# A transformer block on one core: the second norm's tiles turned by DMA in place of TensorE

## The chip, the cores and the metric

The kernel runs on one core of a Trainium2 chip. The metric is the device time of one execution in microseconds (us), the median of several runs. Five engines work side by side, each through its own in-order list of instructions: TensorE (PE; its weight loads are shown apart as PEld), VectorE (DVE), ScalarE (ACT), GpSimd (POOL), and SyncE (SP), which here does nothing but issue DMAs, one after the other.

## The reference, cut to what matters

One pre-norm transformer block in bf16: 2048 rows, width 512, 32 heads of 16, a gated feed-forward of width 1792.

```python
x = A_x                                   # (1, 2048, 512)
h = x + attention(layernorm(x), A_wqkv, A_wo)
h2 = h + glu(layernorm(h))                # the second norm
# glu(y) = (sigmoid(y @ w_gate) * (y @ w_up)) @ w_down
```

`layernorm` subtracts the row's mean and divides by the root of its variance plus 1e-5, with no weights.

## The kernel before, in words

The 2048 query rows are cut into five chunks: chunks 0, 1 and 2 of 512 rows, chunks 3 and 4 of 256. Attention is one long loop of 683 numbered steps. A step computes scores of three (chunk, head group, key block, head) units on PE (line 876) into one of two PSUM buffers `pss`, takes their exponential (line 887, ACT; in some steps VectorE does a third of them by a bit trick, lines 905 to 920), and some steps later multiplies by the values (line 958) into the accumulator `acc`. The keys lie in `KT`, the query rows of a head group in one of two buffers `QB`.

When a head group of a chunk is done, `emit_norm` (line 927) divides by the row sums through a chain of DMAs, all issued by SP: VectorE copies `acc` to `xs` (932), four DMAs take the sums to DRAM (`sd`, 935), one brings them back spread over the partitions (`s_all`, 936), VectorE takes the reciprocal (943) five or six steps later, one DMA writes it to DRAM (`rd`, 945), four broadcast it (`rb_all`, 947), and VectorE multiplies ten or eleven steps after the start (939, into `OT`). SP also issues, in program order between these, the query rows of the next head group (`emit_q_rows`, line 238, four DMAs, and their bounds `bnd`, line 248, two), the loads of x (`xr`, 598) and the output (640). An SP instruction that waits holds up all that stand behind it.

Beside attention, a Python generator `filler()` yields small pieces of other matmul work, which `emit_fill` (line 973) puts behind the scores of chosen steps: `("at", n)` means the next step that is n modulo 4, `("gap", n)` leaves n steps free, `("from", n)` waits for step n. `later(i, fn)` has `fn` emitted at step i. The order of all engines is written out this way; no scheduler changes it.

For chunks 0 to 3 the filler does, while the following chunk's attention runs, the output projection, the second norm and the feed-forward (`ffn_tasks`):

- `ffn_wo` (chunks 0, 1) or `ffn_wo_tight` (chunks 2, 3) takes a tile of 128 rows at a time: eight matmuls (`wo_mm`, line 593) into a `pm` tile, then `wo_ln`, which adds x (602), takes mean and variance (145, 146), has the root taken on POOL (152) and emits the normalization `ln_apply` (156, VectorE) two steps later into the bf16 tile `hn` (tag `xn`, two buffers).
- `hn_transpose` turns the tile: `transpose4` writes four 128x128 transposes by PE (162) into a `pm` tile, and VectorE copies them to `hnT` (163). In the attention phase `pm` has one PSUM buffer, shared by all fillers.
- `ffn_up` multiplies `hnT` by the gate and up weights (617), with a tanh on ACT (622) and a product on VectorE (630). The first gate group reads `hnT` of all the chunk's tiles. `ffn_down` (633, 638) makes the output.

By the built order, the tiles of chunk 0 are turned at steps 193, 201, 209 and 217 and its first gate group stands at step 219; chunk 1: 365, 373, 381, 389 and 391; chunk 2: 533, 537, 541, 545 and 547; chunk 3: 641, 645 and 647. The last chunk (`ffn_last`, after the loop) turns its two tiles by itself (line 786).

Of the kernel before, what the change touches and what calls it, by code (L numbers as in the profile page):

```python
# [19 lines left out]
def kernel(  # L20
# [11 lines left out]
    nc = tc.nc  # L32
    P = 128
# [6 lines left out]
    NG = H // 4  # L40
# [30 lines left out]
    def pm_tile():  # L71
        return pmh["pool"].tile([P, 512], FP32, name="pm")
# [13 lines left out]
    for part in (1, 0, 2):  # L86
        nc.sync.dma_start(out=wqkv_sb[:, :, part * D:(part + 1) * D],
                          in_=wqkv_v[:, :, part * D:(part + 1) * D])
# [3 lines left out]
    hnT = reg[:, o1:o1 + DC * QC].rearrange("p (c q) -> p c q", c=DC)  # L92
# [50 lines left out]
    def ln_stats(src, mv):  # L143
        st = small.tile([P, nc.vector.BN_STATS_DIM], FP32, name="st")
        nc.vector.bn_stats(out=st[:], in_=src)
        nc.vector.bn_aggr(out=mv, in_=st[:])

    def ln_rstd(mvs, n):
        ve = small.tile([P, n], FP32, name="ve")
        nc.vector.tensor_scalar(out=ve[:], in0=mvs[:, :, 1], scalar1=1e-5, scalar2=None, op0=ALU.add)  # L150
        rs = small.tile([P, n], FP32, name="rs")
        nc.gpsimd.tensor_tensor(out=rs[:], in0=ve[:], in1=pw_neg[:, 0:n], op=ALU.pow)  # L152
        return rs

    def ln_apply(dst, src, mv, rs):
        nc.vector.tensor_scalar(out=dst, in0=src, scalar1=mv[:, 0:1], scalar2=rs,
                                op0=ALU.subtract, op1=ALU.mult)

    def transpose4(dst3, src, copy=None):
        pt = pm_tile()[:].bitcast(BF16)[:, 0:4 * P].rearrange("p (b q) -> p b q", b=4)  # L160
        for b in range(4):
            nc.tensor.transpose(out=pt[:, b, :], in_=src[:, b * P:(b + 1) * P], identity=ident_bf[:])
        (copy or nc.vector.tensor_copy)(out=dst3, in_=pt)
# [423 lines left out]
    def tiles_of(c):  # L587
        q0, w = CHUNKS[c]
        return range(q0 // P, (q0 + w) // P)

    def wo_mm(ps, c, tt, g):
        assert ("o", c, g) in ready
        nc.tensor.matmul(ps[:], lhsT=OT[c % 2][:, g, tt * P:(tt + 1) * P], rhs=wo_pad[:, g, :],  # L593
                         start=(g == 0), stop=(g == NG - 1))

    def x_load(t):
        xr = pmh.get("work", work).tile([P, D], BF16, name="xr")
        nc.sync.dma_start(out=xr[:], in_=x_v[:, t, :])
        return xr

    def wo_ln(ps, xr, tt):
        nc.vector.tensor_tensor(out=h_sb[:, tt, :], in0=ps[:], in1=xr[:], op=ALU.add)
        mv = small.tile([P, 1, nc.vector.BN_AGGR_DIM], FP32, name="mv")
        ln_stats(h_sb[:, tt, :], mv[:, 0, :])
        rs = ln_rstd(mv, 1)
        hn = pmh.get("work", work).tile([P, D], BF16, name="xn", tag="xn")
        later(state["step"] + 2, lambda: ln_apply(hn[:], h_sb[:, tt, :], mv[:, 0, :], rs[:, 0:1]))
        return hn

    def hn_transpose(tt, hn, copy=None):  # L610
        transpose4(hnT[:, :, tt * P:(tt + 1) * P], hn, copy)

    def blocks_of(w):
        return [tuple(range(f, f + QC // w)) for f in range(0, FC, QC // w)]
# [24 lines left out]
                                       op0=ALU.mult, op1=ALU.add)  # L639
        nc.sync.dma_start(out=out_v[:, t, :], in_=ob[:])  # L640

    def ffn_wo(c):
        for tt, t in enumerate(tiles_of(c)):
            xr = x_load(t)
            yield ("at", 3)
            ps = pm_tile()
            for g in range(NG):
                if g == NG // 2:
                    yield ("at", 1)
                yield 1  # L650
                wo_mm(ps, c, tt, g)
            hn = wo_ln(ps, xr, tt)
            yield ("gap", 1)
            yield ("at", 1)
            yield 1
            hn_transpose(tt, hn)

    def ffn_wo_tight(c):
        turn = None
        for tt, t in enumerate(tiles_of(c)):  # L660
            xr = x_load(t)
            yield ("at", 3)
            ps = pm_tile()
            for g in range(NG):
                if g == NG // 2:
                    yield ("at", 0)
                yield 1
                wo_mm(ps, c, tt, g)
            hn = wo_ln(ps, xr, tt)
            if turn:  # L670
                yield ("at", 1)
                yield 1
                hn_transpose(*turn)
            turn = (tt, hn)
        yield ("gap", 1)
        yield ("at", 1)
        yield 1
        hn_transpose(*turn)

    def ffn_up(c):  # L680
        w = CHUNKS[c][1]
        at = cycle((3, 1) if c + 2 < NC else (3, 0, 1))
        for fs in blocks_of(w):
            yield ("at", next(at))
            psg = pm_tile()
            for i, f in enumerate(fs):
                for k in range(DC):
                    yield w / QC
                    ffn_mm(wg, psg, w, f, i, k)
            sg = gate_act(psg)  # L690
            yield ("at", next(at))
            psu = pm_tile()
            for i, f in enumerate(fs):
                for k in range(DC):
                    yield w / QC
                    ffn_mm(wu, psu, w, f, i, k)
            up_mul(psu, sg, fs, w)

    def ffn_down(c, tight):
        at = 0  # L700
        for tt, t in enumerate(tiles_of(c)):
            for f in range(FC):
                if tight:
                    if f % 3 == 0:
                        yield ("at", (3, 0, 1)[at % 3])
                        at += 1
                elif f % 5 in (0, 3):
                    yield ("at", 0 if f % 5 else 3)
                if f == 0:
                    psd = pm_tile()  # L710
                yield 1
                down_mm(psd, f, tt)
            down_out(psd, t, tt)

    def ffn_tasks(c):
        tight = c + 3 >= NC
        yield ("rate", 8.0)
        yield from (ffn_wo_tight if tight else ffn_wo)(c)
        yield from ffn_up(c)
        yield from ffn_down(c, tight)  # L720
        yield ("rate", None)
        yield ("gap", 1)
# [102 lines left out]
    def filler():  # L825
        for t in range(NV0, NT):
            yield from fill_v(t)
        for b in range(1, 4):
            yield from fill_k(b)
            yield from fill_q0(b)  # L830
        for qc in range(1, NQC):
            yield from fill_q(qc)
        for c in range(NC - 1):
            yield ("from", int(first_step(c + 1)) + (11 if c + 3 >= NC else 15))
            yield from ffn_tasks(c)
        yield from wo_early(NC - 1)
# [129 lines left out]
    def later(i, fn):  # L966
        due.setdefault(i, []).append(fn)
# [3 lines left out]
    state = {"wait": 0, "debt": 0.0, "done": False, "next": 0, "rate": None}  # L971
# [135 lines left out]
```

## Time and profile before

| | |
|---|---|
| median of 3 runs | 961.85 us (961.81 to 962.77) |
| profiled execution | 963.82 us |
| its span, first to last instruction | 962.0 us |
| mean granted TensorE clock | 0.996 of full |
| the 56 transposes of the fillers (line 162) | 219 ns median each as recorded, pipelined; one group of four 0.38 to 0.40 us |
| the 14 copies (line 163) | 418 ns median each |
| the 14 normalizations (line 156) | 541 ns median each |

A profile line of a timeline reads: start, length, engine, line of the kernel, operation, output<-input, how many; in brackets the idle time of the engine just before and what ended it. A line of a window table reads: start:end of the stretch, its length, then the busy time (and count) of PE, PEld, DVE, ACT and POOL, the granted clock, the DMA share and GB/s. "SPq" is SP issuing a DMA: the duration is that of the issue. In the chain, a piece "DMA" is the time from an issue's start until the work it released went on. Times of a timeline are counted from the span's start.

### The profile page before, as it was taken

The page shows a single profiled execution, that of the slowest core. Times are in us where ns is not written, and L with a number is a line of the kernel's source. Part 1 is how long each engine was busy: PE and PEld are TensorE (multiplying, and loading weights), DVE is VectorE, ACT ScalarE, POOL GpSimd, SP SyncE. Part 2 cuts the span into 40 slices and gives each one's busy share as a digit, 9 for nine tenths or more (in the row PEclk, how much of TensorE's full clock was granted, in tenths as well). Part 3 has the DMA queues.
Part 4 walks back from the last instruction along what each step waited for, and adds up shares of the span by engine and source line. Part 5 has one row for each costly group of instructions (what it writes and reads, how often), then busy time and mean ns, then how long its engine had stood idle before and what let it go on. Part 6 is the DMA issues. An engine that isn't in the chain of part 4 may idle for free.

```text
span 962.0 us, 17291 instructions
## 1 busy us (share of the span) xinstructions
PE 843.0 (88%) x6442; PEld 337.0 (35%) x6442; DVE 782.9 (81%) x1413; ACT 898.6 (93%) x778; POOL 39.8 (4%) x56
## 2 busy tenths in 40 slices
PE   5998888878888999998788999988788999998988
PEld 2321222222222232222222223222355545456646
DVE  7488888888788888899888888898898778777643
ACT  6789999999999999999999999999998999999862
POOL 4600000000000000000000000000000000000000
PEclk9998999999999999999999999999999999999999
DMA  5102450000003000001001000000010000110010
GB/s 161 24 1 56 115 117 16 16 16 3 15 26 103 16 16 17 19 14 30 9 26 27 16 17 15 19 10 27 16 31 23 17 10 16 27 32 16 9 35 12
DMA packets 37645, 28.45 MB, mean 30 GB/s; under 512 B 17788, under 2 KB 32920, under 8 KB 37560
## 3 DMA queue, kind: packets, MB, share of 16 engines
q1 hardware_dynamic: 37416, 27.22, 10.8%
q8 instruction: 50, 0.82, 0.4%
q14 instruction: 35, 0.29, 0.1%
q10 hardware_dynamic: 144, 0.13, 0.0%
HBM read 20.31 MB, written 2.61 MB: 24 GB/s over the span
## 4 chain that ended last, share of the span: by engine, by line
PE 45%; DVE 22%; ACT 22%; issue 6%; DMA 3%; SPq 1%; POOL 0%; ACTq 0%; DVEq 0%
PE pss L876 21%; ACT pt L887 13%; PE acc L958 8%; PE pm L617 7%; ACT stg L887 4%; ACT wd L887 3%; DVE stg L906 2%; PE pm L633 2%; ACT QTu L887 2%; PE pm L593 2%; DVE pt L919 2%; DVE y L915 2%; PE pm L166 1%; DVE reg L909 1%; DVE reg L630 1%
## 5 line engine op out<-in xcount | busy, mean ns | idle before, releaser
L876 PE MATMUL pss<-QB,KT 128*128 128x512 bf16 (+3 forms) x2554 | 477.5, 338 | 80.2 <-ACT pt L887 40.6
L887 ACT ACTIVATE pt<-pss 128x1536 bf16<-128x1536 f32 (+1 forms) x392 | 502.3, 1364 | 17.1 <-PE pss L876 10.6
L876 PEld LDWEIGHTS <-KT 64*128 64x128 bf16 (+1 forms) x2554 | 179.4, 95 | 341.4 <-issue 233.5
L887 ACT ACTIVATE stg<-pss 128x1536 bf16<-128x1536 f32 (+1 forms) x140 | 183.3, 1359 | 5.0 <-PE pss L876 3.8
L906 DVE TENSOR_SCALAR stg<-pss 128x512 int32<-128x512 f32 x123 | 84.8, 690 | 68.2 <-PE pss L876 60.5
L958 PE MATMUL acc<-pt,Vaug 128*17 128x512 bf16 (+1 forms) x1471 | 112.7, 338 | 2.3 <-DVE pt L919 1.2
L887 ACT ACTIVATE wd<-pss 128x1536 bf16<-128x1536 f32 (+1 forms) x80 | 103.9, 1387 | 3.0 <-PE pss L876 2.6
L887 ACT ACTIVATE QTu<-pss 128x1024 bf16<-128x1024 f32 (+1 forms) x71 | 95.7, 1348 | 1.7 <-PE pss L876 1.3
L912 DVE SCALAR_TENSOR_TENSOR y<-reg 128x512 f32<-128x512 f32 x123 | 85.2, 692 | 4.2
L915 DVE SCALAR_TENSOR_TENSOR y<-y,reg 128x512 f32<-128x512 f32 x123 | 84.3, 685 | 1.1
L958 PEld LDWEIGHTS <-Vaug 128*17 128x17 bf16 x2560 | 49.3, 89 | 95.6 <-issue 81.3
L617 PE MATMUL pm<-reg,reg 128*128 128x512 bf16 (+1 forms) x280 | 57.9, 337 | 7.6 <-DVE reg L630 7.5
L617 PE MATMUL pm<-reg,wu 128*128 128x512 bf16 (+1 forms) x280 | 58.1, 338 | 1.4 <-ACT sg L622 1.1
L633 PE MATMUL pm<-wd,reg 128*128 128x512 bf16 x196 | 55.6, 382 | 1.9 <-DVE ob L638 1.9
L909 DVE TENSOR_SCALAR reg<-stg 128x512 int32<-128x512 int32 x123 | 51.9, 422 | 1.8
L958 PE MATMUL acc<-stg,Vaug 128*17 128x256 bf16 (+1 forms) x564 | 50.6, 326 | 0.7 <-DVE stg L919 0.7
L630 DVE SCALAR_TENSOR_TENSOR reg<-sg,pm 128x512 bf16<-128x512 f32 x56 | 38.2, 683 | 14.2 <-PE pm L617 13.8
L919 DVE SCALAR_TENSOR_TENSOR pt<-y,stg 128x512 bf16<-128x512 f32 x70 | 48.0, 686 | 2.0
L152 POOL TENSOR_TENSOR rs<-ve,pw_neg 128x1 f32<-128x1 f32 x16 | 11.7, 734 | 881.9 <-DVE ve L150 875.3
L622 ACT ACTIVATE sg<-pm 128x512 f32<-128x512 f32 x56 | 36.3, 649 | 10.2 <-PE pm L617 9.8
L906 DVE TENSOR_SCALAR wd<-pss 128x512 int32<-128x512 f32 x45 | 31.0, 689 | 17.0 <-PE pss L876 15.5
L171 PE MATMUL pm<-reg 128*128 128x512 bf16 x124 | 38.2, 397 | 1.4 <-DVE stg L521 0.7
(149 smaller groups left out, 718.0 us busy)
## 6 DMA issues: line engine op xcount, KB each, us to landing
rb_all<-rd SPq DMA_DIRECT2D x96, 64.0 KB
xr<-in_A_x_dram SPq DMA_DIRECT2D x16, 128.0 KB
out_dram<-ob SPq DMA_DIRECT2D x15, 128.0 KB
rb_all<-rd SPq DMA_DIRECT2D x60, 32.0 KB
reg<-in_A_x_dram SPq DMA_DIRECT2D x7, 256.0 KB
KT<-stg SPq DMA_DIRECT2D x7, 256.0 KB
reg<-in_B_w_gate_dram SPq DMA_DIRECT2D x4, 448.0 KB
wu<-in_B_w_up_dram SPq DMA_DIRECT2D x4, 448.0 KB
```

The lines of the kernel that those rows point to most:

```text
L171: nc.tensor.matmul(ps[:], lhsT=wqkv_sb[:, c, w0:w0 + P], rhs=xnT[:, c, n * QC:(n + 1) * QC], start=(c == 0), stop=(c == DC - 1))
L617: nc.tensor.matmul(ps[:, i * w:(i + 1) * w], lhsT=wt[:, c, f * P:(f + 1) * P], rhs=hnT[:, c, 0:w], start=(c == 0), stop=(c == DC - 1))
L630: nc.vector.scalar_tensor_tensor(out=out, in0=a, scalar=1.0, in1=b, op0=ALU.add, op1=ALU.mult)
L633: nc.tensor.matmul(ps[:], lhsT=hT[:, f, tt * P:(tt + 1) * P], rhs=wd[:, f, :], start=(f == 0), stop=(f == FC - 1))
L876: nc.tensor.matmul(pss[:, ui, h * w:(h + 1) * w], lhsT=KT[rows, g, kt * P:(kt + 1) * P], rhs=QB[n_qg % 2][rows, j, 0:w], start=True, stop= ...
L887: ex = nc.scalar.activation(out=pt[:, 0:na, :], in_=pss[:, 0:na, :], func=ACT.Exp, scale=DH ** -0.5 / QS)
L906: return nc.vector.tensor_scalar(out=e_bits, in0=src, scalar1=ONE_BITS, scalar2=0.0, op0=ALU.add, op1=ALU.max)
L909: nc.vector.tensor_scalar(out=e_man, in0=e_bits, scalar1=0x7FFFFF, scalar2=-0x40800000, op0=ALU.bitwise_and, op1=ALU.bitwise_or)
L912: nc.vector.scalar_tensor_tensor(out=e_pol, in0=m, scalar=PA, in1=m, op0=ALU.add, op1=ALU.mult)
L915: nc.vector.scalar_tensor_tensor(out=e_pol, in0=e_pol, scalar=PB, in1=e_man.bitcast(FP32), op0=ALU.add, op1=ALU.mult)
L919: nc.vector.scalar_tensor_tensor(out=dst, in0=e_pol, scalar=PC, in1=e_bits.bitcast(FP32), op0=ALU.add, op1=ALU.mult)
L958: nc.tensor.matmul(acc[32 * j:32 * j + VW, 0:w], lhsT=Vaug[:, kt, 4 * g + j, :], rhs=p[:, h * w:(h + 1) * w], start=(kt == 0), stop=(kt == ...
```

## The change

The four transposes of a tile on PE and the copy by VectorE are replaced by four DMAs from SBUF to SBUF that transpose on the way. They are issued by SP, emitted three steps after `wo_ln`, one step after the normalization. `hn_transpose` goes, and with it the filler's waits for its place; the two variants of `ffn_wo` become one. Chunks 0 and 1 leave two free steps after each tile, and every chunk three before the feed-forward. The last chunk and the first norm are not changed.

```diff
         hn = pmh.get("work", work).tile([P, D], BF16, name="xn", tag="xn")
+
+        def turn():
+            for b in range(4):
+                nc.sync.dma_start(out=hnT[:, b, tt * P:(tt + 1) * P], in_=hn[:, b * P:(b + 1) * P], transpose=True)
+
         later(state["step"] + 2, lambda: ln_apply(hn[:], h_sb[:, tt, :], mv[:, 0, :], rs[:, 0:1]))
-        return hn
-
-    def hn_transpose(tt, hn, copy=None):
-        transpose4(hnT[:, :, tt * P:(tt + 1) * P], hn, copy)
+        later(state["step"] + 3, turn)
...
-    def ffn_wo(c):
+    def ffn_wo(c, tight):
         for tt, t in enumerate(tiles_of(c)):
             xr = x_load(t)
             yield ("at", 3)
             ps = pm_tile()
             for g in range(NG):
                 if g == NG // 2:
-                    yield ("at", 1)
+                    yield ("at", 0 if tight else 1)
                 yield 1
                 wo_mm(ps, c, tt, g)
-            hn = wo_ln(ps, xr, tt)
-            yield ("gap", 1)
-            yield ("at", 1)
-            yield 1
-            hn_transpose(tt, hn)
-
-    def ffn_wo_tight(c):
...
+            wo_ln(ps, xr, tt)
+            if not tight:
+                yield ("gap", 2)
+        yield ("gap", 3)
...
-        yield from (ffn_wo_tight if tight else ffn_wo)(c)
+        yield from ffn_wo(c, tight)
```

By the built order of the changed kernel, the transposing DMAs stand on SP at these places: chunk 0, tile 2 directly ahead of the query rows of the next head group; chunk 2, tile 0 ahead of an `rd`, tile 1 ahead of an `xr` and an `sd`, tiles 2 and 3 between `s_all` and `rd`; chunk 3, tile 0 ahead of an `rd`, tile 1 between the next group's `s_all` and its `rd`. The first gate group of chunk 0 moves from step 219 to 223 and that of chunk 1 from 391 to 395; those of chunks 2 and 3 stay at 547 and 647. Lines behind the change move up by 21 in the changed kernel (876 becomes 855).

More of the change, by code (lines that the diff above doesn't have):

```diff
@@ L648, in ffn_wo @@
                 if g == NG // 2:
-                    yield ("at", 1)
+                    yield ("at", 0 if tight else 1)
                 yield 1
                 wo_mm(ps, c, tt, g)
-            hn = wo_ln(ps, xr, tt)
-            yield ("gap", 1)
-            yield ("at", 1)
-            yield 1
-            hn_transpose(tt, hn)
-    def ffn_wo_tight(c):
[L659 to L678, printed above, removed]
+            wo_ln(ps, xr, tt)
+            if not tight:
+                yield ("gap", 2)
+        yield ("gap", 3)
     def ffn_up(c):
```

## The prediction

> **What bounds the kernel now.** I read the page's busy shares first, then its chain, then windows and timelines around the 14 turned tiles.
>
> ```profile
> PE 843.0 (88%) x6442; PEld 337.0 (35%) x6442; DVE 782.9 (81%) x1413; ACT 898.6 (93%) x778; POOL 39.8 (4%) x56
> PE 45%; DVE 22%; ACT 22%; issue 6%; DMA 3%; SPq 1%; POOL 0%; ACTq 0%; DVEq 0%
> ```
>
> No engine alone is the bound: ScalarE (ACT) is 93% busy, and the chain goes through TensorE (PE), VectorE (DVE) and ACT, since two score buffers tie them together. So the answer differs by stage. Windows of one four-step cycle show it (columns: length, then busy us of PE, PEld, DVE, ACT, POOL).
>
> ```profile
> 289.80:294.70 4.90, 4.63 (x32) 1.60 (x32) 3.57 (x8) 4.90 (x5) 0.00 (x0) 1.00 0.37 89
> 716.70:722.60 5.90, 5.25 (x61) 3.21 (x60) 5.46 (x14) 5.29 (x6) 0.59 (x1) 1.00 0.17 44
> 722.60:729.50 6.90, 5.65 (x62) 3.12 (x61) 6.16 (x13) 5.12 (x4) 0.70 (x1) 1.00 0.12 28
> 729.50:734.90 5.40, 4.49 (x56) 2.76 (x55) 5.13 (x11) 5.00 (x4) 0.97 (x1) 1.00 0.02 2
> ```
>
> In chunk 0 (first row, with one turned tile) ACT is busy 4.90 of 4.90: whatever PE and DVE save there is hidden. In chunk 2 two cycles are 0.5 and 1.5 us longer than the 5.4 of their neighbour, with ACT idle.
>
> **What goes.** 56 PE transposes and 14 DVE copies (418 ns each, 5.9 us). The view of line 162 gives the transposes' waits as 4.4 + 2.0 + 1.4 + 0.4 + 0.2 = 8.4 us, and the timeline shows 0.38 to 0.40 us for each group of four, 5.6 us in all. On the path is only what ACT waits for:
>
> ```profile
> 727.09 1.02 PE L593 MATMUL pm<-wo_pad,OT 128*128 128x512 bf16 x4 [1.01 <-DVE reg L163]
> 729.52 1.02 ACT L887 ACTIVATE pt<-pss 128x1024 bf16<-128x1024 f32 x1 [1.42 <-PE pss L876]
> ```
>
> PE waits 1.01 us for the copy of line 163 to give back the one PSUM buffer `pm`, and ACT then idles 1.42 us. I count the chunk-2 excess, 0.5 + 1.5 less 0.1 that ACT needs anyway: 1.9 us gained. In chunks 0 and 1 nothing is gained, since ACT covers it; what could be late next there is ACT itself. In chunk 3 the saved PE time only runs into the wait below, so 0.
>
> **What is moved.** In the built order the FFN of chunks 0 and 1 starts four steps later (219 to 223, 391 to 395) and still ends at steps 324 and 496, ahead of the next filler at 359 and 527. Steps are shifted, not added: 0. If that cover fails, one bad meeting with another task costs the difference between FFN cycles, 6.0 (326.0 to 332.0) against 5.4. FFN steps of chunks 2 and 3 stay.
>
> **What comes.** 56 transposing DMAs of 128x128, four a tile, on SP's in-order queue. No row shows one. Let T be the time from one to the next, whether SP is held or the transfers follow one another, and let the last land 1.40 us after it starts (the chain's piece DMA rd from 736.17). T's lower end is SP's cheapest issue, 0.22 (line 935); the upper end is 1.85, the chain's piece DMA rb_all from 738.87, if each waits out the one before. Nearer rows are the dearest plain issue, 0.62 (line 248: 1.25 for two), and 1.40, a small DMA issued and landed. It cuts more pieces than the former and should not need a full round trip each, so I take their middle, **T = 1.0**. In the Trainium skill, "VectorE: DVE Perf Modes", section "The three transpose paths", a DMA transpose of this tile is put at 1309 ns against 390 on TensorE; no run here shows it, and by it the sum below would be +23.6 instead of +15.6.
>
> SP itself has time for 56 T. What matters is who stands behind them and who waits. Three places come out of the new SP order.
>
> *Place 1, chunk 0.* Tile 2's transposes wait for its normalization (line 156, 300.03 + 0.54), and the next head group's query rows now stand behind them. Before, SP ran ahead:
>
> ```profile
> 292.73 2.48 SPq L238 DMA_DIRECT2D QB<-QTu  x4
> 295.25 1.25 SPq L248 DMA_DIRECT2D QB<-bnd  x2
> 302.15 5.27 ACT L887 ACTIVATE pt<-pss 128x1536 bf16<-128x1536 f32 x4
> ```
>
> The first bound row now lands at 300.57 + 4T + 2.52 + 1.40 = 304.5 + 4T. Step 213's scores need it; its exp is the fourth of the last row, at 302.15 + 3/4 x 5.27 = 306.1, and scores take 0.6. Loss: 4T - 1.0, so 3.0 us. In chunk 1 the rows behind tile 1's transposes would land at 512.9 (end of rb) + 4T + 0.4 (xr) + 2.5 + 1.4 = 521.2, 0.6 of scores ahead of their step's exp at 525.22: some 3 us to spare, 0.
>
> *Place 2, chunk 2.* The order is tile 0's four, rd, rb, QB, tile 1's four, xr, sd, s_all, tile 2's four, tile 3's four. Tile 0's start at 716.11 (line 156), so rd goes at 720.1 instead of 717.68 and everything behind is 2.4 late: tile 1's from 725.16 + 2.4 = 727.6 to 731.6, sd at 732.0 with xr's 0.4 (before: 727.40), s_all done 2.45 later, tile 2's from 734.4, tile 3's from 738.4, the last landed at 738.4 + 3 + 1.4 = 742.8. The first gate matmuls (line 617, 738.15) need it by 738.15 + 0.65. So the chunk ends 4.0 late, the 1.9 gain swallowed; below T of about 0.7 nothing is lost and part of the 1.9 stays.
>
> *Place 3, chunk 3.* Here tile 1's transposes stand behind s_all, which waits for sd to land, which stands behind rb and QB:
>
> ```profile
> 867.75 0.32 SPq L945 DMA_DIRECT2D rd<-r_all  x1
> 869.19 2.20 SPq L947 DMA_DIRECT2D rb_all<-rd  x4
> 871.43 2.47 SPq L238 DMA_DIRECT2D QB<-QTu  x4
> 873.96 1.25 SPq L248 DMA_DIRECT2D QB<-bnd  x2
> 875.31 1.24 SPq L935 DMA_DIRECT2D sd<-xs_all  x4
> 877.42 0.34 SPq L936 DMA_DIRECT2D s_all<-sd  x1
> 875.75 1.05 PE L617 MATMUL pm<-reg,reg 128*128 128x256 bf16 x8
> ```
>
> The last row is the first gate group, which reads both tiles: it runs before s_all is even issued, so these transposes come late whatever they cost. rd waits for tile 0's (866.19 + 4T = 870.2, was 867.75), tile 1's start 10.05 later at 880.2 and the last lands at 880.2 + 3.0 + 1.4 = 884.6, needed by 875.75 + 0.33. PE stands for 8.6 us, with the scores of the following steps queued behind it. There is no cover: the next exp (877.74) already waits for scores that stand behind this gate group. This wait goes to the end in full.
>
> **Sum** at T = 1.0: 3.0 + 4.0 + 8.6 = **+15.6 us**. The profiled execution took 963.8 us (span 962.0 and 1.8 around it), so 979.4; the median shown, 961.85, is 2.0 below that execution, and against it the sum gives **977.5 us**. By the same three formulas T = 0.22 gives 0 - 1.9 + 3.8 = +1.9, T = 0.62 gives 1.5 - 1.7 + 5.9 = +5.7, T = 1.4 gives 4.6 + 10.0 + 11.4 = +26.0, and T = 1.85 gives 6.4 + 16.8 + 14.5 = +37.7.
>
> **Rivals.**
>
> *Cheap transposes (T under 0.62).* A transposing DMA costs what a plain one does. The xr issue, 128 KB in 128 rows, is 0.39; with it the sum is 0.6 - 1.9 + 4.3 = +3.0, so 964.9. For it: SP's plain issues all lie between 0.2 and 0.6. Against: none of them reorders elements of two bytes. The Trainium skill has this rule ("Advanced Engine Details and Errata", section "X-Bar Transpose (TRN2)": transpose DMAs on this chip are as fast as regular ones); no trace here can bear it out. Chance 0.25.
>
> *Dear transposes (T over 1.4),* each waiting out the one before as the rb piece does: up to +37.7, 999.6. Against: plain DMAs of one burst are issued every 0.2 to 0.6 us without waiting. Chance 0.13.
>
> *Faster.* The place is PE in all 14 turns: if PE, not ACT, set the pace there, the 5.6 us of transposes and 8.4 of waits would go in full, 14.0 us, less the two losses at T = 0.39 (0.6 + 4.3): -9.1, 952.8. It decides once more than 4.9 us of it lies on the path. For it: PE's 45% of the chain. Against: ACT's 4.90 of 4.90, and place 3's order, which no T mends. Chance 0.05.
>
> *Not what it says:* the turned tiles stay on PE. The built order shows 56 fewer there and 56 more on SP. Chance 0.02, 961.85.
>
> **How the numbers follow.** The forecast's band (T 0.62 to 1.4, +5.7 to +26.0) has 0.55. Within 0.2% (1.9 us, about what a measurement of this kernel can tell from no change): 0.02 and 0.04 of the cheap case, 0.06. Faster 0.05, slower the remaining 0.89. The range goes from 964 (T near 0.22) to 990 (T near 1.5), leaving out faster, no change and most of the dear case, some 0.2.
>
> **What would show it.** In the profile after: PE's first gate group of chunk 3 waits for a DMA of hnT, 4 to 11 us; chunk 2's gate likewise or not, by T; scores wait for QB near 305 us; SP issues show T. The 1.01 us wait on line 163 is gone. Wrong if chunk 3's gate runs without that wait, or if chunks 0 and 1 get shorter.

## The result, and the profile after

The changed kernel takes **1002.87 us** (median of 4 runs, 1001.53 to 1003.57) against 962.31 for the kernel before on the same chip: a ratio of 1.0416, 95% interval 1.040 to 1.0433. It is slower, as forecast, but by 40.6 us instead of 15.6, and outside the range. Line numbers behind the change are 21 lower than before (scores 855, exponential 866, values 937, `emit_norm`'s DMAs 914 to 926); the transposing DMA is line 610, the gate's matmul 619.

Busy time, granted clock and chain of the profiled execution after (span 1001.0); the last row is the clock before:

```profile
PE 852.4 (85%) x6386; PEld 337.2 (34%) x6386; DVE 779.9 (78%) x1399; ACT 899.3 (90%) x778; POOL 39.9 (4%) x56
PEclk9999999999998999999999999999987999997999
PE 42%; DVE 23%; ACT 21%; issue 6%; SPq 4%; DMA 3%; POOL 0%; ACTq 0%; DVEq 0%
PEclk9998999999999999999999999999999999999999
```

PE has 56 instructions fewer than before and is busy 9.4 us longer (843.0 before). Nothing was added to it, so its matmuls ran slower: the clock row (tenths of full speed, in 40 slices of the span) dips in three places, before's in one, near the start. SP's share of the chain has gone from 1% to 4%. The view of line 610 gives T, the prediction's unknown, as the time that SP is held per transposing DMA (columns: shortest, median, longest in ns, first and last start):

```profile
L610 SPq DMA_TRANSPOSE reg<-xn x56: 1094/1230/1842, 277.7 to 912.8; - x56
```

T is 1.23 us. The last tile's data is there when the gate group's last wait ends, at 915.17 (below): 2.4 us after that DMA's start, where I had assumed 1.40. The waits that were not there before, or grew (columns: total us, times, longest):

```profile
PE pm L619 <- DMA reg<-xn: 14.1, 7, 9.4
DVE OT L918 <- DMA rb_all<-rd: 14.0, 8, 4.3
PEld L619 <- DMA reg<-xn: 10.9, 2, 9.7
DVE reg L602 <- DMA xr<-in_A_x_dram: 7.2, 2, 4.4
PE pss L855 <- DMA QB<-bnd: 4.5, 1, 4.5
```

Only the two on line 619 wait for transposed data (PE and its weight load, PEld, stand idle together there, so the two sums overlap). The others wait for ordinary transfers. Before, `rb_all` was waited for 9.1 us, and neither `xr` nor `QB` at all.

To see where the time comes from I paired the 683 exponentials of the attention loop, step by step, with those of before and took the difference of their starts. (Before's profiled execution lost 2.4 us in the prologue that most others did not lose, so I count from step 60.) By the stretch in which each chunk's FFN runs (steps 60 to 330, to 536, to 640, to the end), in us of lateness gained:

| | chunk 0 | chunk 1 | chunk 2 | chunk 3 |
|---|---|---|---|---|
| predicted | 3.0 | 0 | 4.0 | 8.6 |
| the changed kernel | 10.0 | 5.3 | 12.9 | 14.3 |

One execution's figures scatter by some us: in the profiles of six later runs that leave chunk 1 as it is, it gained 2.0 to 3.9.

**Place 1** is where it was forecast. SP, PE and ACT in chunk 0, from the timeline after:

```profile
301.07 4.92 SPq L610 DMA_TRANSPOSE reg<-xn  x4
306.08 2.47 SPq L238 DMA_DIRECT2D QB<-QTu  x4
308.61 1.26 SPq L248 DMA_DIRECT2D QB<-bnd  x2
310.29 1.01 PE L855 MATMUL pss<-QB,KT 64*128 64x512 bf16 x2 [4.46 <-DMA QB<-bnd]
311.39 1.45 ACT L866 ACTIVATE pt<-pss 128x1536 bf16<-128x1536 f32 x1 [4.85 <-PE pss L855]
```

The query rows stand behind tile 2's four transposes; PE waits 4.46 us for the bounds, ACT 4.85 for PE. The bounds are there 1.68 us after their issue (308.61 to 310.29), not 1.40.

**Place 3** too. In chunk 3 SP waits for `sd` to land before it can issue `s_all`, and tile 1's transposes come after that:

```profile
908.61 0.34 SPq L915 DMA_DIRECT2D s_all<-sd  x1
909.06 4.97 SPq L610 DMA_TRANSPOSE reg<-xn  x4
911.34 0.39 PE L619 MATMUL pm<-reg,reg 128*128 128x256 bf16 x1 [9.41 <-DMA reg<-xn]
915.17 1.23 PE L619 MATMUL pm<-reg,reg 128*128 128x256 bf16 x5 [0.90 <-DMA reg<-xn]
916.19 1.49 PE L855 MATMUL pss<-QB,KT 128*128 128x256 bf16 x6
916.43 0.60 ACT L624 ACTIVATE sg<-pm 128x512 f32<-128x512 f32 x1 [12.95 <-PE pm L619]
```

The gate's first matmul waits 9.41 us, and three of the next wait about 0.9 each, one T less the matmul: 12.1 in all. The scores behind it take 1.49 us instead of 0.82.

**Place 2** is not where chunk 2 loses most. Behind tile 0's transposes stand `rd`, `rb_all` and then a load of x (`xr`), which the prediction's list of this place leaves out. The first two rows are SP before, the next five are after; the last is the sum of a wait after, from 730 to 785:

```profile
719.12 1.71 SPq L947 DMA_DIRECT2D rb_all<-rd  x4
720.87 0.42 SPq L598 DMA_DIRECT2D xr<-in_A_x_dram  x1
729.84 5.65 SPq L610 DMA_TRANSPOSE reg<-xn  x4
737.20 1.72 SPq L926 DMA_DIRECT2D rb_all<-rd  x4
738.96 0.42 SPq L598 DMA_DIRECT2D xr<-in_A_x_dram  x1
741.14 0.69 DVE L602 TENSOR_TENSOR reg<-pm,xr 128x512 f32<-128x512 f32 x1 [4.42 <-DMA xr<-in_A_x_dram]
747.38 1.02 ACT L866 ACTIVATE pt<-pss 128x1024 bf16<-128x1024 f32 x1 [6.42 <-PE pss L855]
PE pm L619 <- DMA reg<-xn: 2.0, 3, 0.8
```

VectorE waits 4.42 us for the load, PE waits behind VectorE, and ACT idles 6.42 us: the lateness grows by 4.8 us from step 536 to 540, ahead of the gate. The gate, which was all of place 2, waits only 2.0 us for transposed data.

**A place that I missed** lies ahead of place 1. VectorE and PE there, and the windows from then on (columns: length, then busy us of PE, PEld, DVE, ACT, POOL, granted clock, DMA share, GB/s):

```profile
287.85 0.25 DVE L922 RECIPROCAL r_all<-s_all 128x16 f32<-128x16 f32 x1 [1.25 <-DMA s_all<-sd]
289.75 0.82 PE L855 MATMUL pss<-QB,KT 128*128 128x512 bf16 x3 [1.43 <-DVE stg L885]
288.50:290.50 2.00, 0.75 (x3) 0.21 (x3) 1.93 (x5) 1.43 (x2) 0.00 (x0) 1.00 0.06 8
290.50:294.00 3.50, 3.50 (x20) 0.87 (x20) 1.76 (x3) 2.65 (x2) 0.00 (x0) 0.54 0.41 94
```

Tile 0's transposes (277.69 to 282.72) hold `sd` back, so the row sums return 1.25 us after VectorE's reciprocal wants them. VectorE is in order: the score bits of line 885 behind it are late, PE idles 1.43 us for their buffer, and then the granted clock is 0.54 for 3.5 us (four matmuls of line 593: 1.78, where the full clock gives 1.04). A wait of 1.25 us on an engine off the path cost 2.7 us. In the profile of a later run that leaves this place as it is (the later gate in chunk 3, below), the wait was 1.0 us, the clock stayed at 1.00 and the loss was 0.9; so most of the 2.7 goes with the clock. With plain DMAs at this place (below) there is neither the wait nor a loss.

### The profile page after: what moved, and what is told of

Its sections match the earlier page's. It is cut to its first block, busy times and chain, and to the rows that moved or that the text cites. A ratio compares the mean times of both kernels' runs of the same rounds, so it can differ in the third digit from the quotient of the medians.

```text
span 1001.0 us, 17237 instructions
## 1 busy us (share of the span) xinstructions
PE 852.4 (85%) x6386; PEld 337.2 (34%) x6386; DVE 779.9 (78%) x1399; ACT 899.3 (90%) x778; POOL 39.9 (4%) x56
## 4 chain that ended last, share of the span: by engine, by line
PE 42%; DVE 23%; ACT 21%; issue 6%; SPq 4%; DMA 3%; POOL 0%; ACTq 0%; DVEq 0%
PE pss L855 19%; ACT pt L866 12%; PE acc L937 7%; PE pm L619 7%; ACT stg L866 4%; ACT wd L866 4%; DVE stg L885 3%; SPq L610 2%; PE pm L635 2%; PE pm L171 2%; DVE pt L898 2%; DVE y L894 2%; PE pm L593 2%; DVE reg L632 2%; ACT QTu L866 2%
## 5 line engine op out<-in xcount | busy, mean ns | idle before, releaser
L619 PE MATMUL pm<-reg,reg 128*128 128x512 bf16 (+1 forms) x280 | 60.6, 344 | 22.2 <-DMA reg<-xn 14.1
L619 PE MATMUL pm<-reg,wu 128*128 128x512 bf16 (+1 forms) x280 | 60.4, 348 | 0.9 <-ACT sg L624 0.7
L885 DVE TENSOR_SCALAR wd<-pss 128x512 int32<-128x512 f32 x45 | 31.0, 689 | 17.1 <-PE pss L855 15.6
L619 PEld LDWEIGHTS <-reg 128*128 128x128 bf16 x280 | 24.6, 98 | 51.0 <-issue 28.6
```

The lines of the kernel that those rows point to most:

```text
L619: nc.tensor.matmul(ps[:, i * w:(i + 1) * w], lhsT=wt[:, c, f * P:(f + 1) * P], rhs=hnT[:, c, 0:w], start=(c == 0), stop=(c == DC - 1))
L885: return nc.vector.tensor_scalar(out=e_bits, in0=src, scalar1=ONE_BITS, scalar2=0.0, op0=ALU.add, op1=ALU.max)
```

## The experiments

All times are medians of 4 to 11 runs, with the ratio to before on the same chip and its interval. Differences between two edited kernels compare different chips; before's median went from 961.96 to 963.17 among them. "Lateness" is read as above, from the one profiled execution.

**What the removal is worth.** The DMAs are replaced by one VectorE copy a tile, without transposition:

```diff
-            for b in range(4):
-                nc.sync.dma_start(out=hnT[:, b, tt * P:(tt + 1) * P], in_=hn[:, b * P:(b + 1) * P], transpose=True)
+            nc.vector.tensor_copy(out=hnT[:, :, tt * P:(tt + 1) * P], in_=hn[:].rearrange("p (b q) -> p b q", b=4))
```

> The changed kernel with the four transposing DMAs of a tile replaced by one VectorE copy of the normalized tile into hnT, emitted at the same step; it leaves the transposition out, so that only the removal and the moved feed-forward are left. Theory A (the loss is made by what waits behind SP's transposing DMAs): the removal alone gains the 1.9 us of chunk 2, so about 960 us, 958 to 963, granted clock back at 0.99. Theory B (the moved feed-forward, or PE with less work and so a lower clock, makes the loss): above 975 us, clock near 0.975.

Measured: 965.72 (ratio 1.004, 1.0025 to 1.0055). The expected gain is not there; it is a loss of nearly 4 us. The profile has it in chunks 0, 1 and 2 (0.6, 1.9 and 2.6). Two suspects: the fillers' order, which the change moves, and the removal itself. So the same copy in before's own order:

```diff
     def hn_transpose(tt, hn, copy=None):
-        transpose4(hnT[:, :, tt * P:(tt + 1) * P], hn, copy)
+        nc.vector.tensor_copy(out=hnT[:, :, tt * P:(tt + 1) * P], in_=hn[:].rearrange("p (b q) -> p b q", b=4))
```

> The kernel before in its own order, but the four transposes on TensorE and their psum buffer are taken out and VectorE copies the norm's tile straight into hnT (transposition left out; VectorE's copies stay, from SBUF). It differs from the copy experiment only in where the fillers stand: here the FFN stays at its steps, there it comes some steps later as in the changed kernel. Theory A (the removal itself gains 1.9 us, and the moved order, which the prediction held to be free, takes it back and 3 us more): 959 to 961. Rival (with TensorE's transposes gone its clock or another wait takes the gain back whatever the order): 962 to 967.

Measured: 962.30 (1.0005, 0.9989 to 1.0021). So the moved order, which I had at 0, costs 3.4 us (965.72 less 962.30; some 1.3 to 5.5 by the two intervals), and the removal itself gains nothing. The windows in chunk 2, this run and then before:

```profile
726.00:730.00 4.00, 2.16 (x24) 1.32 (x25) 3.83 (x9) 0.85 (x2) 0.50 (x1) 0.89 0.12 34
730.00:734.00 4.00, 4.00 (x44) 1.98 (x42) 3.31 (x9) 2.49 (x3) 0.95 (x1) 0.68 0.02 3
726.00:730.00 4.00, 2.99 (x31) 1.59 (x30) 3.49 (x7) 2.58 (x3) 0.04 (x1) 1.00 0.16 38
730.00:734.00 4.00, 3.40 (x51) 2.21 (x50) 3.75 (x9) 3.62 (x4) 0.97 (x1) 1.00 0.02 3
```

PE is idle longer (2.16 busy of 4.00, before 2.99), and the clock falls to 0.89 and 0.68; before had 1.00 in both. What comes first in this trace is a wait on SP (the first two rows are this run, the next two before; the last two are waits of this run):

```profile
716.49 0.32 SPq L945 DMA_DIRECT2D rd<-r_all  x1
719.84 1.71 SPq L947 DMA_DIRECT2D rb_all<-rd  x4
717.68 0.32 SPq L945 DMA_DIRECT2D rd<-r_all  x1
719.12 1.71 SPq L947 DMA_DIRECT2D rb_all<-rd  x4
DVE reg L602 <- DMA xr<-in_A_x_dram: 1.9, 1, 1.9
PE acc L958 <- DVE xs_all L932: 2.2, 1, 2.2
```

`rb_all` needs `rd`, and goes 3.35 us after it instead of 1.44. The load of x stands behind it; VectorE waits 1.9 us for the load and PE 2.2 us for VectorE, which before did not, and then the clock falls. The profile of the first copy experiment has the same slow `rd` (3.58). So there are two candidates for what took the gain, this late load and the clock behind it. Four matmuls on constants now stand where the transposes stood, to keep PE busy:

```diff
+        pt = pm_tile()
+        for b in range(4):
+            nc.tensor.matmul(pt[:, b * P:(b + 1) * P], lhsT=ident_bf[:], rhs=ident_bf[:], start=True, stop=True)
         nc.vector.tensor_copy(out=hnT[:, :, tt * P:(tt + 1) * P], in_=hn[:].rearrange("p (b q) -> p b q", b=4))
```

> The kernel before in its own order with VectorE's straight copy instead of the transposition (transposition left out), as in the order experiment, and four matmuls of 128 columns on constants where each tile's transposes stood, whose result no one reads. Theory A (TensorE's clock, which falls once it has stood idle where the transposes were, took the gain back): the granted clock stays at 1.00 from 726 to 734 us and the time is 959.5 to 961. Rival (the gain was never there: another wait, such as that for acc or xr, ends at the same time): 961.8 to 963, whatever the clock.

Measured: 961.17 (0.9993, 0.9983 to 1.0002): unclear, between the two. The granted clock is 1.00 in all windows from 718 to 742, and the lateness after step 60 is -0.7 us where it was +0.9 without these matmuls. But `rb_all` follows `rd` by 1.44 us again, and VectorE does not wait for `xr`. So the run does not tell the clock from the late load, and the time can't tell the rest of 0.7 us from no change.

**Transposing or moving?** Plain DMAs of the same blocks at the same place in SP's queue (transposition left out):

```diff
-                nc.sync.dma_start(out=hnT[:, b, tt * P:(tt + 1) * P], in_=hn[:, b * P:(b + 1) * P], transpose=True)
+                nc.sync.dma_start(out=hnT[:, b, tt * P:(tt + 1) * P], in_=hn[:, b * P:(b + 1) * P])
```

> The changed kernel with plain DMAs of the same 128x128 blocks at the same places of SP's queue; it leaves the transposition out. Theory A, with the time from one to the next as the plain DMA's issue, about 0.4 us: place 1 0.6, place 2 -1.9, place 3 4.3 plus about 2 for a slow clock after the wait, so 965 to 969 us, chunk 3's gate still waiting 3 to 5 us. Theory C (any four DMAs at these places cost as much, the order alone decides): about 1000 us.

Measured: 980.26 (1.0177, 1.0149 to 1.0204), between the theories.

```profile
L610 SPq DMA_DIRECT2D reg<-xn x56: 465/599/1352, 280.0 to 890.8; - x56
890.75 0.39 PE L619 MATMUL pm<-reg,reg 128*128 128x256 bf16 x1 [5.19 <-DMA reg<-xn]
```

T is 0.60, and still 18 us are lost: 5.19 in one wait at chunk 3's gate, the rest mostly in chunks 0 and 2, at places where the changed kernel loses too (4.3 and 5.3 us of lateness). My formulas gave +5.7 for T = 0.62. So the price of a DMA was not the only thing wrong: nearly half the loss comes with any 56 DMAs put there.

**By chunk.** Transposing DMAs in chunks 0 and 1 alone, and in 2 and 3 alone, the others as before:

```diff
...
-        yield from (ffn_wo_tight if tight else ffn_wo)(c)
+        if c in (0, 1):                       # the other run: (2, 3)
+            yield from ffn_wo_dma(c, tight)
+        else:
+            yield from (ffn_wo_tight if tight else ffn_wo)(c)
```

> Transposing DMAs in chunks 0 and 1 alone; chunks 2 and 3 as before, on TensorE. Theory A: what the changed kernel had lost by step 496 of the loop, 13.9 us, so about 976 us (974 to 979). My prediction's three places would give 3 to 4 us, 966. Theory B: about half of the whole, 982.

> Transposing DMAs in chunks 2 and 3 alone; chunks 0 and 1 as before. Theory A: the rest of the loss, 39.0 - 13.9 = 25 us, so about 987 us (984 to 990), and with the run of chunks 0 and 1 alone the parts add up to the whole. If they add up to clearly less than 39, the chunks share a cause such as the clock.

Measured: 974.94 (1.0144, 1.0124 to 1.0164) and 986.24 (1.025, 1.0235 to 1.0266), both as expected from the first profile: 13.0 and 24.3, 37.3 of the 40.6. The halves nearly add up.

**The queue or the data?** Before, with its own transposes on PE, plus 56 transposing DMAs into a buffer that nothing reads:

```diff
+    dead = const.tile([P, 2, P], BF16, name="dead")
...
+        def turn():
+            for b in range(4):
+                nc.sync.dma_start(out=dead[:, b % 2, :], in_=hn[:, b * P:(b + 1) * P], transpose=True)
+        later(state["step"] + 3, turn)
```

> The kernel before with TensorE's transposes and VectorE's copies kept, plus the same 56 transposing DMAs from the same tiles, issued three steps after the norm's statistics, into a buffer that no one reads. Nothing waits for them but what stands behind them on SP's queue. Theory A (SP's queue is the larger part in chunks 0 to 2, the wait for the transposed data the larger part in chunk 3): chunks 0 and 1 cost about the 13 us that they cost alone, chunk 2 some 5 to 8, chunk 3 little, in all 979 to 985. Rival (the data's own lateness is the price everywhere): 962 to 968. Rival (the queue is the price everywhere, chunk 3 too): 998 to 1003.

Measured: 1007.47 (1.0458, 1.0435 to 1.0482), above all theories. Its waits:

```profile
DVE OT L946 <- DMA rb_all<-rd: 24.3, 9, 6.2
DVE reg L604 <- DMA xr<-in_A_x_dram: 19.0, 7, 6.2
```

No one needs the turned data, and the loss is 45 us. What stands behind the DMAs is enough for all of it: `rb_all` (9.1 us of waits before) and `xr` (none). This is an upper bound, since two halves of one buffer made some groups of four hold SP for up to 6.5 us instead of 5.0.

The counterpart: all the loop's other DMAs leave SP for GpSimd's queue, in before (the control) and in the changed kernel.

```diff
-        nc.sync.dma_start(out=xr[:], in_=x_v[:, t, :])     # likewise QB's rows and bounds, sd, s_all, rd, rb_all
+        nc.gpsimd.dma_start(out=xr[:], in_=x_v[:, t, :])
```

> The kernel before with the loads of xr, the QB rows and bounds and the four steps of the norms' DMAs (sd, s_all, rd, rb_all) issued from GpSimd's queue instead of SP's. The control of the next run. GpSimd is busy for 4% of the span, so both theories expect a time near that of before: 960 to 975, the more the longer one issue on GpSimd takes than the 0.3 to 0.6 us on SP.

> The changed kernel with the same DMAs on GpSimd's queue, so that the transposing DMAs have SP's queue nearly to themselves. Theory A (the price is what stands behind the transposing DMAs on SP's queue; the transposed data itself is late only because those stand behind the others): at most 5 us above its control, with the waits on QB<-bnd, xr and rb gone and the wait for transposed tiles in chunk 3 under 3 us. Rival (a transposing DMA slows the other DMAs, or its data lands late, whatever the queue): 20 us or more above the control.

Measured: 1015.40 and 1023.63. The control itself is 53 us slower than before, which I had not expected. Its profile shows longer waits inside the norms' chain (VectorE's for `s_all` 43.7 us in all instead of 4.3, for `rb_all` 27.4 instead of 9.1); why the chain is slower from this queue stays open. Between the two the transposing DMAs cost 8.2 us instead of 40.6. With the queue to themselves they leave these waits:

```profile
PEld L619 <- DMA reg<-xn: 4.3, 2, 3.3
PE pm L619 <- DMA reg<-xn: 3.4, 3, 2.1
```

The waits on `xr` and `QB` are down to 1.0 and 0.2 us, and those for transposed data to 7.7 of 25.0 (sums of two rows that overlap). Neither "at most 5" nor "20 or more" was met, but this and the run before point to the queue. A slower control may hide some of the price, so 8.2 is not what a free queue would leave here.

**The places one by one.** In chunk 0 tile 2's transposes are issued three steps later, behind the query rows:

```diff
-        later(state["step"] + 3, turn)
+        later(state["step"] + (6 if late else 3), turn)   # late: chunk 0, tile 2
...
```

> The changed kernel, but in chunk 0 tile 2's four transposing DMAs are issued three steps later, so that the next group's QB rows and bounds are issued ahead of them instead of behind. Theory A (place 1 is blocking on SP's queue and its lateness stays to the end): lateness at steps 212 to 216 goes from 6.8 to under 1 us, and the time falls by 6 to 7 us to 996 to 997. Rival (the lateness would be swallowed by later slack, or only moves to the transposes): 1001 to 1004.

Measured: 995.63 (1.0338, 1.0318 to 1.0359), 7.2 less. The order on SP, and no wait on QB any more:

```profile
297.92 2.46 SPq L238 DMA_DIRECT2D QB<-QTu  x4
300.43 1.26 SPq L248 DMA_DIRECT2D QB<-bnd  x2
...
302.30 4.98 SPq L610 DMA_TRANSPOSE reg<-xn  x4
```

In chunk 3 the gate comes four steps later:

```diff
-        yield ("gap", 3)
+        yield ("gap", 7 if c == 3 else 3)
```

> The changed kernel with the fillers' pause between chunk 3's last output matmul and its first gate matmul four steps longer (7 instead of 3), so that the gate comes some 5 us later and its tiles have more time. Theory A (the wait of 9.4 us is the distance between gate and transposes, and can be bought by distance): the wait falls to 3 to 5 us and the time by 4 to 6 us, to 997 to 999. Rival (the fillers behind it have no slack either, and end later by what the wait gave): 1001 to 1005.

Measured: 993.70 (1.0324, 1.0305 to 1.0342), 9.2 less, more than the 4 to 6 I expected.

```profile
911.40 1.23 PE L619 MATMUL pm<-reg,reg 128*128 128x256 bf16 x5 [0.90 <-DMA reg<-xn]
```

Its first matmul no longer waits 9.4 us; four steps' scores now run ahead of it, and only waits of 0.40, 0.91 and 0.90 are left. Of chunk 3's 14.3 us, 7.5 stay; so chunk 3 accounts for 6.7 of the 9.2, and the rest lies in stretches that the edit does not touch.

For chunk 2, `xr` loaded one tile earlier (in every chunk), and, in another run, chunk 2's gate four steps later. The edit of the first:

```diff
-            xr = x_load(t)
+            xr = xrs.pop(0)       # filled with two loads at the start, then one a tile
...
```

> The changed kernel, but each input tile xr is loaded one tile earlier, so that in chunk 2 no load stands behind the reciprocals and the transposes. Theory A (the place that the prediction missed: L602 waits 4.4 us for xr): the waits of L602 on xr go, the 4.8 us of lateness at steps 536 to 540 go, and the time falls by 4 to 6 us to 997 to 999. Rival (chunk 2 is held by the transposed tiles themselves, so that an earlier xr is given back at the gate): 1001 to 1003.

> The changed kernel with the fillers' pause ahead of the gate four steps longer in chunk 2 alone. Theory A (a good part of chunk 2's lateness is the gate that waits for the last tiles' transposes, and TensorE's slow clock after that wait): the lateness that arises at steps 544 to 560, 8 to 10 us, falls to 2 to 4 and the time by 5 to 7 us, to 996 to 998. Rival (chunk 2's lateness is the wait for xr and the norms' DMAs behind the transposes, which a later gate doesn't touch): 1001 to 1004.

Measured: 1003.19 (1.042, 1.0402 to 1.0439) and 998.09 (1.0362, 1.0347 to 1.0378). The first theory falls: at steps 536 to 540 the lateness gained went from 4.8 to 2.2 us, but it came back at and behind the gate (steps 544 to 560: 12.5 us instead of 8.7; in all 13.4 us in chunk 2, 12.9 in the changed kernel). With the later gate the time is 4.8 us less. Its wait in chunk 2 goes, but this comes instead:

```profile
750.08 11.33 SPq L610 DMA_TRANSPOSE reg<-xn  x8
761.51 0.53 SPq L924 DMA_DIRECT2D rd<-r_all  x1
766.28 0.43 DVE L918 TENSOR_TENSOR OT<-xs_all,rb_all 128x256 bf16<-128x256 f32 x1 [6.20 <-DMA rb_all<-rd]
```

Eight transposes hold SP for 11.3 us, `rd` stands behind them, and VectorE waits 6.20 for `rb_all`. Chunk 2 still loses 16.0 us, 10.3 of them at steps 544 to 560, so the theory fails here too. What this run gained shows up in chunk 3 (8.6), where the gate's first wait is 3.85 us instead of 9.41, and the edit was not made for that.

Then two combinations: chunk 0's edit with the later gate in chunks 2 and 3, and with that of chunk 3 alone.

> The changed kernel with tile 2's transposes of chunk 0 three steps later and the pause ahead of the gate four steps longer in chunks 2 and 3, all three at once. Theory A (the places are independent): 7 us from chunk 0 and 9 from chunk 3, as measured one by one, and what the run with chunk 2 alone gains, 5 to 7: 979 to 983. Rival (places share lateness, so that one bought off is paid at the next): 986 to 993.

> The changed kernel with tile 2's transposes of chunk 0 three steps later and the pause ahead of the gate four steps longer in chunk 3 alone; chunk 2 as it was. Theory A (chunks 0 and 3 are independent, and the run with all three moved fell back because chunk 2's later end pushed chunk 3's two tiles into one block of eight transposes): 7.2 and 9.2 us less than the changed kernel's 1002.9, 985 to 988. Rival (what is bought in chunk 0 is paid in chunk 3): 991 to 996.

Measured: 996.13 (1.0347, 1.0328 to 1.0366) and 990.50 (1.030, 1.0283 to 1.0317). The first is no better than one edit alone. Chunk 2's later end pushes chunk 3's two tiles together:

```profile
897.51 10.07 SPq L610 DMA_TRANSPOSE reg<-xn  x8
913.70 0.43 DVE L918 TENSOR_TENSOR OT<-xs_all,rb_all 128x256 bf16<-128x256 f32 x1 [10.85 <-DMA rb_all<-rd]
```

The second gains 12.4 us of the 16.4 that the two edits gained singly. It lies between the bands, 2.5 us above theory A's and 0.5 below the rival's: most of the two gains add, and some of the lateness may be shared. Its profiled execution, at 988.7, is the fastest of its four. An edit must not move another place's DMAs into a block, as the first combination did.

**The clock after a wait.** 36 matmuls that no one reads stand ahead of chunk 3's gate:

```diff
             psg = pm_tile()
+            if c == 3 and fs[0] == 0:
+                spin(psg, wo_pad[:, 0, :], 36)
```

> The changed kernel with 36 matmuls of 512 columns that no one reads put ahead of chunk 3's first gate matmul, where TensorE otherwise stands idle for 9.4 us. They fit inside the wait (36 x 0.22 = 7.9 us). Theory A (a TensorE that has stood idle is granted a clock of 0.50 for some us after, which the price of chunk 3 holds beside the wait itself): the wait for the transposed tile stays, but the scores behind it (L855 x6) fall from 1.49 to about 0.82 us and the gate's x8 from 1.71 to about 1.03, and the time by 1.5 to 2.5 us, to 1000.5 to 1001.5. Rival (the wait alone is the price): 1002.5 to 1004, the matmuls behind the wait as slow as before.

Measured: 1001.80 (1.0405, 1.0388 to 1.0422), inside the scatter of the changed kernel. It lies between the two theories and does not decide: PE still idled for 2.9 us after the added matmuls and three times 0.9, and ran the scores behind at half speed again. That a slow clock follows the waits is seen in each trace; how much of the 40.6 us it makes was not isolated. An estimate from the two pages: PE was busy 9.4 us longer although some 5.6 us of transposes went, so its matmuls took some 15 us more, of which only a part can lie on the path.

No version beat the kernel before, and no experiment points to one: even at no price for the transposition the removal gains nothing that can be measured.

## Why the prediction was wrong, step by step

- *Direction, and places 1 and 3: right.* Both waits stand where the order on SP put them, and moving the DMAs apart removed them (7.2 and 9.2 us).
- *T = 1.0, landing 1.40:* T is 1.23 us; the last transposed tile landed 2.4 us after its DMA's start, the bounds of place 1 1.68 after theirs. With these the three formulas give 4.2 + 8.5 + 11.2 = 23.9 us (place 1: 4 x 1.23 - 1.0 + 0.3; places 2 and 3 by their slopes between T = 1.0 and 1.4, plus 1.0). So both sizes were too small; by the formulas they make 8.3 us of the miss. At step 213 in chunk 0 the lateness grows by 4.95 us, for 4.2; there the exponential starts 1.1 us after its first score matmul, where I had 0.6. The Trainium skill ("VectorE: DVE Perf Modes", "The three transpose paths") has 1309 ns for a DMA transpose, and the trace comes close with 1230. The sum by that price, +23.6, misses the time as well. The Trainium skill's rule that transposing DMAs are as fast as regular ones ("Advanced Engine Details and Errata", "X-Bar Transpose (TRN2)") does not hold here for the time on the queue: 1230 ns against 599 for the same blocks at the same place.
- *"Three places":* the step that failed. I followed the query rows and the gate, and priced `rd` and `sd` only as a shift of the last transposes; for VectorE's own waits the sum had nothing. VectorE is in order too and waits for `s_all`, `rb_all` and `xr`; PE and ACT then wait for VectorE. Tile 0 in chunk 0 cost 2.7 us this way. In chunk 2 my list of SP's order left out the load of x behind `rb_all` (720.87 before), and VectorE's wait for it cost 4.8 us ahead of the gate; the gate itself waited 2.0 us for transposed data, where the formula has 8.5. Chunk 2 loses 13 to 16 us whichever of its waits is taken away. With DMAs that no one reads the loss was as large.
- *"What is moved: 0":* 3.4 us.
- *The gain of 1.9 us in chunk 2:* it did not come (962.30 against 962.35); a late load of x and a slower clock stand in its place in the trace. The sum at T = 1.0 held no gain (place 2 swallows it), so this explains nothing of the miss.
- *A wait costs its length:* it cost more. In chunk 3 the waits sum to 12.1 and the lateness to 14.3; in chunk 0 place 1 shows 4.95 and then 1.7 more with slow scores.
- *"Faster", 8.4 us of waits at line 162:* this sum takes PE and its weight loads together; PE itself waited 1.8 us of it. The forecast does not use it.

Of the 16.7 us between 23.9 and 40.6, the moved order makes about 3.4, if it adds to the rest, and the missed place in chunk 0 makes 2.7. The other 10.6 are spread over the four chunks. In the traces they go with VectorE's waits and the slow clock behind a wait; the runs do not separate these two.

## What to carry to other kernels

When DMAs join an in-order queue, list everything that stands behind each of them until the queue has caught up, and for each the engine that waits for it and what stands behind that engine's wait; the data of the new DMA itself is only one entry. A place is cleared by distance (a later gate, an earlier load) only if the same edit moves no other DMA into a block. Work taken from an engine that is not the bound can gain nothing even where others waited for it: look at which wait ends next there, the landing of a DMA included, and at the clock behind it.

## What the runs showed of the hardware

- A transposing DMA of 128x128 bf16 from SBUF to SBUF holds its issuing queue for 1.23 us, a plain one of the same block 0.60.
- TensorE's granted clock fell to 0.54 after a 2.0 us stretch in which PE was busy 0.75 us, and stayed low for 3.5 us. The Trainium skill ("TensorE: Matmul & The Clock Gate", Part 1) gives half rate after an idle window of some 3.4 us; here the longest idle stretch ahead of it was 1.43 us. At the same place in another execution, after a wait of VectorE of 1.0 us instead of 1.25, the clock stayed at 1.00.
- SP issues `rb_all` when `rd` has landed, at the median 1.43 us after `rd`'s issue, before as in the run with the copy in before's order. In each of the two profiles three of 39 took 2.2 to 3.4 us, at different places in the two. The cause stays open.
- Issued from GpSimd, the loop's ordinary DMAs made the kernel before 53 us slower. The cause stays open.
